# A fused attention and two mixture layers on one core: more loads in flight at once, and a new order and engine choice under that plan

## The chip, the cores and the metric

The kernel runs on one core of a Trainium2 chip. The metric is the device time of the whole kernel in microseconds (us). A profiled execution also gives the span: the time from the first to the last recorded instruction. The core has TensorE (PE; its weight loads are listed as PEld), VectorE (DVE), ScalarE (ACT), GpSimd (POOL) and SyncE (SP), which in this kernel issues every transfer; the transfers run on 16 DMA engines.

## The reference

```python
# 1. attention, q, k, v of (4, 8, 576, 64), two results added
q_d, k_d, v_d = means of q, k, v over 4 neighbouring tokens        # 144 tokens
out_up    = repeat(softmax(q_d @ k_d.T / 8) @ v_d, 4)
out_local = softmax(q @ k.T / 8 where |i - j| < 4) @ v
x = out_up + out_local                                             # as 2304 tokens x 512
# 2. a layer with a rational function
h = x @ w_in                                                       # 512 -> 2048
P = a[0] + a[1] * h + a[2] * h * h + a[3] * h * h * h
Q = 1.0 + abs(b[0]) * abs(h) + abs(b[1]) * h * h
x = (P / (Q + 1e-06)) @ w_out                                      # 2048 -> 512
# 3. soft mixture of 8 experts, 4 slots each
logits = x @ phi                                                   # 32 slots
slot_input = softmax(logits, over the tokens).T @ x
slot_out   = relu(slot_input @ w1[e]) @ w2[e]                      # 8 experts, 512 -> 1024 -> 512
out = softmax(logits, over the slots) @ slot_out
```

The softmax over the tokens needs all 2304 tokens before the first expert can start, so the experts form a tail behind everything else.

## The kernel before

**Stages.** The attention is done for 16 pairs of heads (four batches of four). A pair needs one load of its q and k (`in_qk`, 579 KB, all 128 partitions) and two of v, always issued one behind the other: `in_vd` (320 KB, for the means) and `in_vw` (560 KB, windows for the local part). There are four sets of buffers. The first batch uses all four; the later pairs wait for one to come free. A pair's q and k are summed over four tokens (L560 on VectorE, or L562 and twice L564 on POOL), its scores are multiplied (L580 local, L590 means), their maxima taken (L595), the exponentials done (ScalarE), divided by their sums (L617), turned, multiplied with v (L643), and added (L667). v is summed by L570 and L571. The result x is split into a high half XH (L729 on ScalarE or L731 on VectorE) and a low half XL = x - XH (L734), because TensorE's products take the rounded type and are made as high x high, high x low and low x high.

The weights `w_in` and `w_out` come as 64-bit floats, eight loads of 1024 KB each, and are narrowed to 32 bits on VectorE (L756, L761, L765). Each part of `w_in` is split into W high and low (the same L729, L731 and L734). Each part of `w_out` is stored as 32 bits to a scratch in DRAM (`wo_dram`, 512 KB), to be loaded again in the tail, and multiplied by phi, so that the logits come straight from the gate.

Products m = 0 to 31 (24 matmuls each, L889) multiply 512 tokens with 256 columns of `w_in`; m = 32 to 35 (L907, 48 matmuls each) do the last 256 tokens with 512 columns. Product m needs XH and XL of its batch and W of its part, and it writes into one of two pairs of PSUM banks, m modulo 2. So product 2 needs the banks that the gate of product 0 has read. A gate is a chain of some ten instructions on 128 x 1024 values: L965 to L994 on ScalarE, VectorE and POOL; the last is L994. Its result is turned (L1018), copied (L729 or L731), and goes into the logits (L1034), and once per 256 tokens into the slots (L1090). The experts follow (L1330, L1451) with 32 loads `we` of 1024 KB, which are issued as buffers come free.

The other loads are two constants at the start, `in_cb` (117.5 KB) and `in_cf` (195 KB).

**What sets the order.** The program is written by a planner. `at` collects items (a part's name, what it reads and writes); every item has a number in the table `PLACE`, and `simulated` (L321) goes through the items in the order of these numbers, so the numbers alone set the order on every engine. For several kinds of item, a letter in the table `F` says which engine takes each instance: d is VectorE, p is POOL, a, s and r are ScalarE, and f is VectorE too, with another place for a result (see g below). The letters of the parts: `pq`, `pk`, `pv` are the sums of q, k, v; `nl`, `nd` are L617; `wil` is the low half of W, `xl` of x; `cr`, `v`, `a`, `t` are steps of the gate (`cr` and `a` are L967 if not on ScalarE, `v` and `t` are L971); `g` = f writes the last but one value of the gate over PSUM, where d writes it to SBUF; `gc` is the copy after L1018.

`simulated` also gives each item a time, from the table of costs `PARTS`. These times decide three things in the program that is built. First, loads are throttled: for a load of the front (`GATED`, q and k, v, `w_in`, `w_out`), it goes back over the loads ahead and adds up their planned durations until `LIMIT` is reached; the load then waits for the landing of the one at which it got there (L352 to L358, built in `begin`, L425). Second, a wait of TensorE that is planned longer than 0.6 us is filled with dummy matmuls (L386; `fillers`, L1157: wide ones at L1159, narrow ones at L1162). Third, of certain instructions on POOL and VectorE the plan lets only one engine's run at a time, and a POOL instruction that is planned right behind one of VectorE waits for it in the program (L434). When a load's data may be used in the plan is `end[n]` at L363; the program itself waits for the data and not for that time.

```python
for m in reversed(loads if part in GATED else ()):
    if ahead >= LIMIT:
        t, self.gate[n] = max(t, end[m] + .1), m
        break
    ahead += items[m][2][0]
```

## Time and profile before

| | |
|---|---|
| time, median of 3 runs | 506.7 us (501.92 to 507.81) |
| profiled execution, its time | 502.77 us |
| profiled execution, span | 501.0 us |
| busy: TensorE | 474.4 us (95%) |
| busy: VectorE | 399.7 us (80%) |
| busy: ScalarE | 322.1 us (64%) |
| busy: GpSimd | 250.6 us (50%) |
| moved by DMA | 88.50 MB, mean 177 GB/s |

The busy times are of the profiled execution. Dummy matmuls count as busy TensorE. The rows that follow the diff come from this execution; a row of a timeline gives the start, the duration, the engine, the line, the operation, what goes out and in, and in brackets how long the engine was idle before it and who released it.

### The profile page before, as it was taken

The page shows a single profiled execution, that of the slowest core. Times are in us where ns is not written, and L with a number is a line of the kernel's source. Part 1 is how long each engine was busy: PE and PEld are TensorE (multiplying, and loading weights), DVE is VectorE, ACT ScalarE, POOL GpSimd, SP SyncE. Part 2 cuts the span into 40 slices and gives each one's busy share as a digit, 9 for nine tenths or more (in the row PEclk, how much of TensorE's full clock was granted, in tenths as well). Part 3 has the DMA queues.
Part 4 walks back from the last instruction along what each step waited for, and adds up shares of the span by engine and source line. Part 5 has one row for each costly group of instructions (what it writes and reads, how often), then busy time and mean ns, then how long its engine had stood idle before and what let it go on. Part 6 is the DMA issues. An engine that isn't in the chain of part 4 may idle for free.

```text
span 501.0 us, 13108 instructions
## 1 busy us (share of the span) xinstructions
PE 474.4 (95%) x5505; PEld 345.4 (69%) x5505; DVE 399.7 (80%) x558; ACT 322.1 (64%) x676; POOL 250.6 (50%) x223
## 2 busy tenths in 40 slices
PE   8798699999999999999999999999989989999995
PEld 5576477677777777766777777777766878543575
DVE  5985989998997888889978988889879988825333
ACT  4584297686968887568688667869585567720223
POOL 3786579466883775575154376723544134301000
PEclk9799799999999999999999999999999999999998
DMA  8997816477654220144301222660202049999988
GB/s 318 296 316 249 301 49 169 160 207 246 211 160 126 47 67 7 41 123 121 104 18 38 86 75 75 205 262 0 85 0 63 22 152 386 381 404 426 427 336 306
DMA packets 17611, 88.50 MB, mean 177 GB/s; under 512 B 2065, under 2 KB 2577, under 8 KB 10897
## 3 DMA queue, kind: packets, MB, share of 16 engines
q1 hardware_dynamic: 17552, 87.67, 50.3%
q8 instruction: 43, 0.70, 0.6%
q14 instruction: 16, 0.12, 0.1%
HBM read 78.75 MB, written 8.91 MB: 175 GB/s over the span
## 4 chain that ended last, share of the span: by engine, by line
PE 50%; DVE 17%; DMA 13%; POOL 8%; ACT 6%; issue 4%; SPq 0%; DVEq 0%; POOLq 0%; ACTq 0%
PE hps L889 18%; DMA at<-in_vw 4%; POOL gate L971 4%; PE gt L1018 4%; PE op L1451 3%; DMA wo_dram<-wo 3%; DVE gate L990 3%; PE hp L1330 3%; POOL W L734 2%; PE lg L1034 2%; PE hps L907 2%; ACT hps L989 2%; PE dsp L1090 2%; DMA wst<-in_w_out 2%; PE av L643 2%
## 5 line engine op out<-in xcount | busy, mean ns | idle before, releaser
L889 PE MATMUL hps<-XH,W 128*128 128x512 f32 x512 | 170.1, 402 | 7.4 <-ACT XH L729 3.0
L889 PEld LDWEIGHTS hps<-XH,W 128*128 128x128 f32 x512 | 97.1, 190 | 33.8 <-ACT XH L729 3.2
L971 POOL TENSOR_TENSOR gate<-gate 128x1024 f32<-128x1024 f32 (+1 forms) x37 | 86.4, 2335 | 59.1 <-ACT gate L976 41.4
L889 PE MATMUL hps<-XL,W 128*128 128x512 f32 x256 | 100.9, 394 | 1.3 <-POOL XL L734 1.3
L967 POOL TENSOR_SCALAR gate<-gate,cf_sb 128x1024 f32<-128x1024 f32 (+1 forms) x25 | 30.7, 1229 | 78.6 <-ACT gate L975 78.6
L990 DVE SCALAR_TENSOR_TENSOR gate<-gate,hps 128x1024 f32<-128x1024 f32 (+1 forms) x37 | 44.0, 1190 | 23.3 <-ACT hps L989 21.3
L988 ACT ACTIVATE gate<-gate,one 128x1024 f32<-128x1024 f32 (+1 forms) x37 | 42.1, 1138 | 29.6 <-POOL gate L971 29.3
L889 PEld LDWEIGHTS hps<-XL,W 128*128 128x128 f32 x256 | 48.6, 190 | 10.8 <-POOL XL L734 1.8
L989 ACT ACTIVATE hps<-gate 128x1024 f32<-128x1024 f32 (+1 forms) x37 | 37.4, 1010 | 14.9 <-DVE gate L987 7.7
L729 ACT COPY G<-gt 128x512 f32<-128x512 f32 x50 | 29.3, 588 | 6.6 <-PE gt L1018 6.5
L1159 PE MATMUL lg<-zero 128*96 128x256 f32 x114 | 31.8, 420 | 1.0 <-DVE zero L1154 1.0
L971 DVE TENSOR_TENSOR gate<-gate,hps 128x1024 f32<-128x1024 f32 x24 | 29.0, 1209 | 3.7 <-ACT gate L965 3.7
L975 ACT ACTIVATE gate<-hps 128x1024 f32<-128x1024 f32 (+1 forms) x26 | 25.9, 996 | 8.2 <-PE hps L889 7.7
L1018 PE MATMUL gt<-cf_sb,gate 128*128 128x128 f32 x192 | 28.7, 279 | 1.3 <-ACT DC L1084 0.9
L994 DVE SCALAR_TENSOR_TENSOR gate<-gate 128x1024 f32<-128x1024 f32 x17 | 28.3, 1663 | 0.4
L965 ACT ACTIVATE gate<-hps,cf_sb 128x1024 f32<-128x1024 f32 x23 | 27.9, 1212 | 1.1 <-PE lg L1034 1.1
L987 DVE SCALAR_TENSOR_TENSOR gate<-gate,cf_sb,hps 128x1024 f32<-128x1024 f32 x22 | 28.0, 1275 | 0.5
L602 ACT ACTIVATE at<-sc,at 128x38 f32<-128x38 f32 x144 | 28.1, 316 | 0.5
L756 DVE TENSOR_SCALAR nar<-wst 128x512 int32<-128x512 int32 (+1 forms) x26 | 21.0, 812 | 8.5 <-DMA wst<-in_w_in 6.2
L617 POOL TENSOR_TENSOR at<-at 128x342 f32<-128x342 f32 (+1 forms) x29 | 23.9, 834 | 6.2 <-DVE at L613 3.7
L1018 PEld LDWEIGHTS gt<-cf_sb,gate 128*128 128x128 f32 x192 | 21.3, 141 | 8.2 <-issue 3.6
L1159 PEld LDWEIGHTS lg<-zero 128*96 128x96 f32 x114 | 19.3, 179 | 10.7 <-issue 3.9
(177 smaller groups left out, 1018.0 us busy)
## 6 DMA issues: line engine op xcount, KB each, us to landing
we<-in_w SPq DMA_DIRECT2D x32, 1024.0 KB, 12.4
at<-in_qk SPq DMA_DIRECT2D x16, 579.0 KB, 4.8
at<-in_vw SPq DMA_DIRECT2D x16, 560.0 KB, 6.4
wst<-in_w_in SPq DMA_DIRECT2D x8, 1024.0 KB, 6.7
wst<-in_w_out SPq DMA_DIRECT2D x8, 1024.0 KB, 6.1
at<-in_vd SPq DMA_DIRECT2D x16, 320.0 KB, 5.0
out<-late SPq DMA_DIRECT2D x17, 256.0 KB, 2.7
wo_dram<-wo SPq DMA_DIRECT2D x8, 512.0 KB, 7.3
```

The lines of the kernel that those rows point to most:

```text
L602: nc.scalar.activation(out=dst[:, i, :], in_=st["s", j][:, i, :], func=ACTF.Exp, scale=scale, bias=mx[:, i:i + 1], accum_out=None if sums ...
L729: nc.scalar.copy(out=out, in_=x)
L889: nc.tensor.matmul(hps[m][:, c].rearrange("p u t -> p (u t)"), lhsT=W[p][:, w, kk, 128 * c:128 * c + 128], rhs=x[xx][:, kk, :], start=(kk ...
L967: (nc.vector if who == "d" else nc.gpsimd).tensor_scalar(out=out, in0=x, scalar1=coef[:, w:w + 1], scalar2=coef[:, b:b + 1], op0=ALU.mult, ...
L971: turned_over((nc.vector if who == "d" else nc.gpsimd).tensor_tensor(out=out, in0=x, in1=y, op=op), who)
L987: stt(out=A, in0=A, scalar=coef[:, 1:2], in1=H, op0=ALU.add, op1=ALU.mult))
L988: do("ln", "C", "B", lambda C, B: act(out=C, in_=B, func=ACTF.Ln, bias=one))
L989: do("ex", "H", "C", lambda H, C: act(out=H, in_=C, func=ACTF.Exp, scale=-1.0))
L990: do("e", "B", "H", lambda B, H: stt(out=B, in0=B, scalar=1.0 + 1e-6, in1=H, op0=ALU.add, op1=ALU.mult))
L994: do("g", "A", "B" + n, lambda A, B, n: turned_over(stt(out=A, in0=B, scalar=-2.0, in1=n, op0=ALU.add, op1=ALU.mult), "d"), pick=("g", m))
L1018: nc.tensor.transpose(gt[n][:, u, 128 * c:128 * c + 128], g_of(n, c)[:, 128 * u:128 * u + 128], idn)
L1159: nc.tensor.matmul(fill[0:96], lhsT=wide, rhs=wide[:, 0:1].to_broadcast([128, TB]), start=not used, stop=True, skip_group_check=True)
```

## The change

`LIMIT` goes from 2.6 to 4.5, the planned time from a transfer's end to the use of its data goes from 0.5 to 0.9, and the table `PLACE` (all of it) and fifteen strings of `F` are new. Nothing else in the program is touched.

```diff
-    pq="dppddpppppdpdddp",
-    pk="ddppppppdpppdpdd",
-    pv="pppppppppppppppp",
-    nl="ppppppppppppppdp",
-    nd="pppppppppppddppp",
+    pq="dppppppppdpppppp",
+    pk="pddppppppppppppp",
+    pv="pppppppppdpdpppp",
+    nl="ppppppppddddppdp",
+    nd="pppppppppdppdppd",
     wih="aaaaaaad",
-    wil="pppppppp",
-    xh="aaaaaadaddaaaaaaa",
-    xl="ppppppppddpppppdp",
-    cr="aspppspssppppppssspppppsspppsppsppppa",
-    t="dpddppddddddddddddddddddddddddddddddd",
-    sd="rsssrsrsrsrrrsss",
-    v="ppppppppppppppppppppppppppppppppppppp",
-    a="aaaaaaaaaaaaaadaaaaaddaaaaaaaaaaaaaaa",
-    g="fdfddffddfdddfddddfddddddddddddddffff",
-    gc="aaaadaaadaadaaaadaaaaddaaadadaaddaaadaaaadaddadaaadaadadadadadaaaaaaaada",
+    wil="pppppppd",
+    xh="aaaaaaaadadadadda",
+    xl="ppppdpdddpppddddd",
+    cr="spppspppppppssppaappdpppppssspappsppa",
+    t="dpdpddddddddddddddddpdddddddddddddddd",
+    sd="rsssssrrssrsssrs",
+    v="pppppppppppppppppdppdppppppppppppdppp",
+    a="aaaaaadaaadaaaaaaaaaaaaaadaaaddaaadaa",
+    g="ddfdfffddddddddddddddffddddddddddddff",
+    gc="aaaaaaaaaadddaaaaadaaaaadadadadaaaaaadadadaadaaaaaaaaaadaadaaaadaaaaadaa",
...
-    ldi=(11, 27, 109, 113, 151, 189, 192, 205),
...
+    ldi=(15, 57, 93, 117, 145, 192, 169, 201),
...
-BACK, LIMIT, GATED = 2.5, 2.6, ("ldqk", "ldv", "ldi", "ldo")
+BACK, LIMIT, GATED = 2.5, 4.5, ("ldqk", "ldv", "ldi", "ldo")
...
-                end[n] = moved + .5
+                end[n] = moved + .9
```

Counted over the strings and the orders of both programs, VectorE gets seven L734 (five XL, the low half of the last W, the low half of the last 256 tokens), five L617, two pairs L570/L571, four L967 and three L971 from other engines, and gives away nine L560 and four L731.

**SP, the loads of the front.** The rows are the stretch around the last v loads of the first batch. at_89 and at_87, at_103 and at_101, at_96 and at_94 are the two v loads of a pair, wst the 64-bit weights, and at_86 the q and k of the fifth pair of heads. Before:

```order
L427 DMA wst_523<-in_w_out 128x2048
L427 DMA wo_dram_71<-wo_423 128x1024
L427 DMA wst_567<-in_w_in 128x2048
L427 DMA at_89<-in_vd 80x1024
L427 DMA at_87<-in_vw 112x1280
L427 DMA wst_577<-in_w_in 128x2048
L427 DMA at_96<-in_vd 80x1024
L427 DMA at_94<-in_vw 112x1280
L427 DMA wst_690<-in_w_in 128x2048
L427 DMA wo_dram_71<-wo_631 128x1024
L427 DMA at_86<-in_qk 128x1158
```

And now:

```order
L427 DMA at_89<-in_vd 80x1024
L427 DMA at_87<-in_vw 112x1280
L427 DMA wst_449<-in_w_out 128x2048
L427 DMA at_103<-in_vd 80x1024
L427 DMA at_101<-in_vw 112x1280
L427 DMA wo_dram_71<-wo_429 128x1024
L427 DMA wst_520<-in_w_in 128x2048
L427 DMA wst_578<-in_w_in 128x2048
L427 DMA at_86<-in_qk 128x1158
L427 DMA wst_642<-in_w_in 128x2048
L427 DMA at_96<-in_vd 80x1024
L427 DMA at_94<-in_vw 112x1280
```

The last pair of v loads (at_96, at_94) stood behind two `w_in` of this piece, with a third `w_in` and the fifth pair's q and k behind it; now the third `w_in` and these q and k stand ahead of it.

**POOL, from the low half of W2 on to that of W4.** XL is the low half of x, at_102, at_88 and at_95 are x of three of the four pairs of the first batch, and L562, L564 sum the q or the k of one of the next pairs. Before:

```order
L734 TENSOR_TENSOR W2_750<-wst_567,W2_750 128x1024
L734 TENSOR_TENSOR XL_544<-at_88,XH_521 128x512
L562 TENSOR_TENSOR at_88<-at_86 128x144
L564 TENSOR_TENSOR at_88<-at_88,at_86 128x144 x2
L734 TENSOR_TENSOR XL_544<-at_95,XH_521 128x512
L734 TENSOR_TENSOR W3_849<-wst_577,W3_849 128x1024
L734 TENSOR_TENSOR W4_891<-wst_690,W4_891 128x1024
```

And now:

```order
L734 TENSOR_TENSOR W2_645<-wst_520,W2_645 128x1024
L562 TENSOR_TENSOR at_88<-at_86 128x144
L564 TENSOR_TENSOR at_88<-at_88,at_86 128x144 x2
L570 TENSOR_TENSOR at_96<-at_96 72x512
L571 TENSOR_TENSOR at_93<-at_96 72x256
L734 TENSOR_TENSOR XL_542<-at_102,XH_540 128x512
L734 TENSOR_TENSOR W3_790<-wst_578,W3_790 128x1024
L734 TENSOR_TENSOR XL_542<-at_88,XH_540 128x512
L734 TENSOR_TENSOR XL_542<-at_95,XH_540 128x512
L734 TENSOR_TENSOR W4_869<-wst_642,W4_869 128x1024
```

The sums at_88 stood between two XL of the first batch, and now stand ahead of all three; one XL more and the sums of v (L570, L571) have come into this piece, and W3 stands ahead of the last two XL.

**TensorE, between the products 1 and 2.** lg<-zero are the fillers, L576 to L590 are the scores of the fifth pair, L832 and L842 the products of `w_out` with phi. Before, the rows right behind the last matmul of product 1:

```order
L1159 MATMUL lg_73<-zero_114 96x256 x5
L842 MATMUL wq_926<-cf_sb_74,pp_580 128x32 x2
L1159 MATMUL lg_73<-zero_114 96x256 x5
L576 LDWEIGHTS cb_sb_75
L576 MATMUL sc_942<-cb_sb_75 128x342
L580 MATMUL sc_942<-at_86 32x38 x36
L832 MATMUL wp_995<-wo_631,cf_sb_74 32x256 x4
L1159 MATMUL lg_73<-zero_114 96x256 x5
L1162 LDWEIGHTS zero_114
L1162 MATMUL lg_73<-zero_114 96x192
L590 MATMUL scd_1006<-at_88 64x144 x6
L1159 MATMUL lg_73<-zero_114 96x256 x7
```

And now, the rows up to the first matmul of product 2 (hps_1011):

```order
L576 LDWEIGHTS cb_sb_75
L576 MATMUL sc_934<-cb_sb_75 128x342
L580 MATMUL sc_934<-at_86 32x38 x36
L832 MATMUL wp_975<-wo_580,cf_sb_74 32x256 x4
L1159 MATMUL lg_73<-zero_114 96x256 x5
L1162 LDWEIGHTS zero_114
L1162 MATMUL lg_73<-zero_114 96x192
L842 MATMUL wq_1002<-cf_sb_74,pp_994 128x32 x2
L1159 MATMUL lg_73<-zero_114 96x256
L889 MATMUL hps_1011<-XH_540,W2_645 128x512
```

Where 22 wide fillers stood in four lots behind product 1 (the turn of the first gate, L1018, and product 2 follow a few narrow ones later), there are six now, and two more stand some rows ahead, inside product 1. The scores L590 of the fifth pair have moved ahead of the end of product 1.

## Rows read from the trace of the kernel before

**Rows 1.** The page: busy tenths in 40 slices of the span, one engine.
```profile
PE   8798699999999999999999999999989989999995
```

**Rows 2.** By stretch: length; PE, PEld, DVE, ACT, POOL busy; clock, DMA share, GB/s.
```profile
0.00:46.30 46.30, 39.11 (x700) 28.49 (x701) 36.59 (x64) 27.66 (x97) 30.84 (x49) 0.93 0.90 294
...
0.00:78.50 78.50, 66.78 (x971) 48.90 (x972) 62.31 (x108) 45.59 (x125) 52.03 (x61) 0.91 0.74 246
78.50:394.20 315.70, 310.31 (x3493) 231.56 (x3491) 275.78 (x343) 233.53 (x475) 178.93 (x151) 1.00 0.34 107
440.00:480.00 40.00, 38.50 (x430) 18.50 (x432) 14.09 (x50) 6.52 (x16) 1.86 (x1) 1.00 1.01 424
```

**Rows 3.** The same by stretch, line L1159 alone: PE, PEld, clock, DMA share, GB/s.
```profile
0.00:78.50 78.50, 23.00 (x82) 14.67 (x82) 0.91 0.74 246
```

**Rows 4.** The same by stretch, fillers of both widths: PE, clock, DMA share, GB/s.
```profile
0.00:78.50 78.50, 24.24 (x95) 0.91 0.74 246
78.50:394.20 315.70, 5.91 (x27) 1.00 0.34 107
```

**Rows 5.** Loads issued on SP (count, first and last start), and the last one's time to landing.
```profile
L427 SPq DMA_DIRECT2D we<-in_w x32: 327/332/729, 318.6 to 467.2; - x32
...
L427 SPq DMA_DIRECT2D wst<-in_w_in x8: 328/328/347, 2.8 to 57.0; - x8
...
wst<-in_w_in SPq DMA_DIRECT2D x1, 1024.0 KB, 5.2
```

**Rows 6.** Timeline of TensorE: the first matmuls of product 2 and of product 32.
```profile
78.55 0.48 PE L889 MATMUL hps<-XH,W 128*128 128x512 f32 x1
...
394.24 1.46 PE L907 MATMUL hps<-xs,W 128*128 128x256 f32 x10 [0.18 <-DVE gate L993]
```

**Rows 7.** VectorE by stretch, then three places of its timeline.
```profile
0.00:78.00 78.00, 61.81 (x107) 0.91 0.75 247
...
5.10 2.21 DVE L560 TENSOR_REDUCE at<-at 128x144 f32<-128x576 f32 x3 [3.57 <-DMA at<-in_qk]
...
50.60 0.69 DVE L756 TENSOR_SCALAR nar<-wst 128x512 int32<-128x512 int32 x1 [4.07 <-DMA wst<-in_w_in]
...
76.80 1.22 DVE L994 SCALAR_TENSOR_TENSOR gate<-gate,hps 128x1024 f32<-128x1024 f32 x1
```

**Rows 8.** Timeline of POOL.
```profile
47.17 1.08 POOL L734 TENSOR_TENSOR XL<-at,XH 128x512 fp32r<-128x512 f32 x1
...
54.68 0.56 POOL L562 TENSOR_TENSOR at<-at 128x144 f32<-128x144 f32 x1 [6.42 <-DMA at<-in_qk]
...
56.51 1.09 POOL L734 TENSOR_TENSOR XL<-at,XH 128x512 fp32r<-128x512 f32 x1
```

**Rows 9.** The chain that ended last, in order of time: start, share of it in us.
```profile
31.31 7.92 DMA at<-in_vw
39.60 6.66 DMA at<-in_vw
```

**Rows 10.** Timeline of VectorE, two of its XL.
```profile
210.87 0.69 DVE L734 TENSOR_TENSOR XL<-at,XH 128x512 fp32r<-128x512 f32 x1
...
324.63 2.45 DVE L734 TENSOR_TENSOR XL<-at,XH 128x512 fp32r<-128x512 f32 x1 [0.55 <-ACT XH L729]
```

**Rows 11.** Groups by line and form: busy us, mean ns of one | idle before.
```profile
L971 DVE TENSOR_TENSOR gate<-gate,hps 128x1024 f32<-128x1024 f32 x24 | 29.0, 1209 | 3.7 <-ACT gate L965 3.7
...
L734 POOL TENSOR_TENSOR W<-wst,W 128x1024 fp32r<-128x1024 f32 x8 | 19.4, 2424 | 4.2 <-ACT W L729 3.4 <-DVE W L731 0.8
L731 DVE COPY G<-gt 128x512 f32<-128x512 f32 x22 | 15.0, 684 | 0.9 <-PE gt L1018 0.8
...
L967 DVE TENSOR_SCALAR gate<-hps,cf_sb 128x1024 f32<-128x1024 f32 x1 | 1.3, 1334 | 0.0
```

**Rows 12.** VectorE by stretch around the small instructions on the coefficients: busy, clock, DMA share.
```profile
19.40:21.10 1.70, 1.63 (x9) 0.70 0.98 242
54.70:56.10 1.40, 1.23 (x8) 0.50 0.89 193
```

More of the change, by code (lines that the diff above doesn't have):

```diff
@@ L160 @@
[L160 to L176 removed]
+    dm=(8,),
@@ new lines @@
+    ldqk=(4, 7, 31, 5, 125, 252, 361, 452, 546, 592, 716, 795, 822, 941, 1027, 1069),
+    ldc=(6, 0),
+    ldv=(42, 76, 163, 72, 219, 413, 466, 551, 602, 722, 800, 862, 944, 1063, 1092, 1176),
+    coef=(1,),
+    roots=(2,),
+    rooted=(3,),
+    pq=(9, 25, 58, 22, 149, 285, 412, 465, 580, 638, 726, 806, 842, 942, 1031, 1117),
+    pk=(10, 21, 81, 16, 174, 335, 383, 453, 554, 617, 748, 796, 858, 960, 1033, 1134),
+    sc=(17, 24, 44, 27, 236, 331, 437, 510, 585, 634, 744, 816, 895, 972, 1040, 1116),
@@ new lines @@
+    w1=(34, 62, 90, 112, 133, 150, 161, 178, 204, 198, 207, 187, 217, 227, 269, 279, 313, 318, 362, 357, 407, 409,
+        449, 469, 542, 547),
+    w2=(46, 63, 109, 118, 134, 165, 164, 179, 205, 200, 214, 191, 225, 230, 276, 281, 314, 319, 363, 369, 414, 420,
+        455, 470, 545, 548),
+    wih=(73, 114, 147, 184, 210, 218, 232, 244),
+    wil=(98, 122, 154, 189, 216, 224, 239, 245),
+    ldo=(20, 74, 246, 294, 327, 387, 436, 492),
+    sto=(80, 235, 282, 349, 405, 450, 500, 628),
+    wt0=(95, 231, 288, 330, 370, 435, 496, 565),
@@ new lines @@
+    wc0=(96, 237, 291, 333, 374, 438, 497, 570),
+    wt1=(88, 128, 292, 326, 379, 424, 503, 562),
+    wc1=(89, 131, 297, 339, 382, 425, 507, 566),
+    wp=(102, 240, 300, 340, 396, 441, 518, 588),
+    wpp=(105, 253, 308, 345, 397, 445, 522, 607),
+    wq=(120, 254, 321, 364, 415, 509, 557, 608),
+    wpc=(121, 257, 324, 367, 419, 513, 563, 619),
+    h=(113, 202, 212, 213, 177, 197, 222, 233, 262, 260, 315, 303, 351, 348, 410, 381, 447, 456, 532, 543, 597, 595,
+        615, 614, 649, 651, 676, 669, 710, 712, 747, 749, 781, 784, 826, 846, 912, 908, 918, 919, 955, 958, 991, 994,
+        1013, 1020, 1048, 1056, 1093, 1090, 1160, 1149, 1197, 1195, 1222, 1221, 1238, 1243, 1259, 1261, 1289, 1288,
+        1299, 1301, 1329, 1325, 1341, 1344),
@@ new lines @@
+    L=(665, 847, 965, 1049, 1256, 1322, 1429, 1477, 1513),
+    mx=(675, 834, 968, 1061, 1251, 1314, 1437, 1471, 1517),
+    al=(733, 874, 1018, 1147, 1278, 1328, 1454, 1479, 1525),
+    E=(692, 848, 1030, 1153, 1266, 1330, 1450, 1482, 1519),
+    ss=(736, 1017, 1034, 1260, 1313, 1355, 1472, 1510, 1528),
+    tk=(729, 849, 1042, 1173, 1277, 1338, 1452, 1483, 1520),
+    dt=(730, 852, 1044, 1174, 1279, 1347, 1459, 1484, 1522),
+    ds=(807, 872, 1045, 1185, 1296, 1350, 1464, 1485, 1523),
+    ac=(810, 880, 1047, 1207, 1297, 1357, 1467, 1499, 1526),
@@ new lines @@
+    wor=(1194,),
+    h8=(1366, 1367, 1365, 1369, 1384, 1385, 1387, 1388, 1420, 1421, 1417, 1418, 1433, 1434, 1441, 1447),
+    we=(1224, 1411, 1391, 1368, 1371, 1489, 1508, 1487, 1509, 1386, 1389, 1422, 1419, 1435, 1449, 1448, 1540, 1542,
+        1524, 1515, 1533, 1555, 1551, 1553, 1549, 1562, 1564, 1569, 1567, 1572, 1580, 1575),
+    zm=(1415,),
+    gst=(1527,),
+    inv=(1529,),
+    gt0=(1530,),
+    gt1=(1531,),
+    sl=(1532,),
+    si0=(1534,),
+    si1=(1535,),
+    si=(1536,),
+    z=(1537,),
@@ L187 @@
[L187 to L193 removed]
+    c2=(1545,),
+    c3=(1546,),
+    cs=(1548, 1560, 1558, 1552, 1563),
+    ct=(1557, 1561, 1583, 1577, 1571),
+    cc=(1566, 1568, 1592, 1582, 1573),
@@ new lines @@
+    l2=(1578, 1579, 1581, 1584, 1585, 1586, 1587, 1588, 1590, 1591, 1594, 1603, 1604, 1610, 1616, 1619, 1597, 1598,
+        1613, 1620, 1627, 1635, 1636, 1644),
+    os=(1589, 1629, 1648),
+    s4=(1593, 1633, 1649),
+    s4h=(1595, 1637, 1650),
+    s4l=(1596, 1638, 1653),
+    o=(1609, 1599, 1606, 1614, 1600, 1612, 1617, 1626, 1624, 1639, 1642, 1647, 1654, 1656, 1658, 1662, 1669, 1665,
+        1667),
+    out=(1623, 1607, 1621, 1625, 1602, 1630, 1632, 1641, 1631, 1645, 1646, 1652, 1657, 1661, 1664, 1666, 1673, 1672,
+        1674),
```

197 lines of the change are left out of this document (65 added, 132 removed), and 14 rows, old and new, of tables (gc, tr).

## The prediction

> **What bounds the kernel now.** I read the page first, then the engines by stretch, then the waits of the front, then the filler matmuls. The slices [rows 1] show TensorE busy nearly everywhere. That row is to be distrusted, because the plan puts dummy matmuls (L1159, L1162) into TensorE's planned waits. The stretches [rows 2] and the fillers alone [rows 3, 4] correct it. Up to 78.5 us TensorE is busy for 66.8 us, but 24.2 of them are fillers of both widths [rows 4], most of them wide [rows 3]: it does 42.5 us of work, and 36 us are waiting, filled or not. From 78.5 to 394.2 us it waits 5.4 us (315.7 less 310.31) and burns 5.9 us of fillers [rows 4]: 11.3 us in 315.7, so this stretch belongs to TensorE, with VectorE close behind at 275.8 us (87%). Behind 394.2 us the loads of the last weights decide: DMA is busy throughout between 440 and 480 us, at 424 GB/s [rows 2], and the last of the 32 loads is issued only at 467.2 us [rows 5].
>
> So the place to look is the front, up to the moment when product 2 starts (78.55 us [rows 6]), just after the first gate is finished (the L994 that begins at 76.80 us [rows 7]). Three things stand there. DMA is the slower side until the last input weight has landed (the eighth load of in_w_in is issued at 57.0 us and takes 5.2, so 62.2 [rows 5]), but busy for only 90% of the first 46.3 us [rows 2]. VectorE works 61.8 of the first 78.0 us [rows 7] and so waits 16.2 us, the longest time 4.07 us for an input weight [rows 7]. And POOL waits 6.42 us at L562 for the q and k of the fifth head pair, with the last XL of the first batch (56.51 us, needed by products 0 and 1) queued behind it [rows 8].
>
> **The loads.** LIMIT goes from 2.6 to 4.5, so a 1 MB load waits for the third load before it instead of the second. The bytes hardly change. What must have moved when the last in_vw of the front lands (39.60 + 6.66, 46.3 us [rows 9]) is, by the sizes in the section on the kernel and the order of SP: before, cb and cf, 4 in_qk, 4 in_w_in, 2 in_w_out, 4 v pairs, one store, 12,804 KB; now one in_w_in and one in_qk more, 14,407 KB, 12.5% more. At the old pace that is 52.1 us; with the DMA never idle (share 0.90 up to 46.3 us [rows 2]) it is 52.1 x 0.90 = 46.9 us. Neither is shown, so I take the middle, 49.5 us, and keep both ends. The same for the last input weight: 17,479 KB in place of 17,991, so 60.4 us at the old pace, 54.4 without idle, 57 taken, against 62.2. A v load needed 9 us from landing (31.31 + 7.92) to the end of its XL (47.17 + 1.08) [rows 8, 9], which gives the last XL at 58.5 us against 57.6 now. The order of POOL keeps the fifth pair's L562 ahead of XL, but its load now stands ahead of the last v, so XL waits for its own data and no more for that one.
>
> **VectorE up to product 2.** The order shows 105 instructions ahead of the first L994 both times: two L560 fewer (three took 2.21 at the start [rows 7], 0.74 each), one L595 more (taken as much as one of them), and the low half of W7 on VectorE, which no row has; twice an XL of 0.69 [rows 10] is 1.4, and POOL's 2.42 for it [rows 11] is the upper end. Together -0.74 + 1.4, +0.7. Against that, the first gate no longer writes into the PSUM of product 0 (g is "d", not "f"), so product 2 needs not wait for L994 itself, 1.22 us. VectorE thus has 61.8 + 0.7 - 1.2 = 61.3 us to do. Its waits: 16.2 now. Thirteen small instructions on the coefficients (1.63 and 1.23 us of VectorE with a neighbour's share, taken as 2.6 [rows 12]) move from busy places to the start, where VectorE waits for its first q and k anyway; and I let half of the 4.07 us wait go. That leaves 16.2 - 2.6 - 2.0 = 11.6, so product 2 starts at 72.9, say 73: **5.5 us won**. Ends: 8 won if the whole 4.07 goes and the DMA never idles; 2 if it keeps the old pace and XL ends at 61. The fillers between products 1 and 2 fall from 22 wide ones to 8 in the order; 14 at 0.56 us (82 records in 23.00 us [rows 3]; a filler is two of them, so 41) are 7.9 us, much the same. I do not count that again.
>
> **From product 2 to product 32.** The order has no filler left between them, 5.9 us before. It also has more VectorE work there, by [rows 11] unless said: three L971 (1.21), four L967 (1.33), five XL (0.69 [rows 10]), five L617 (taken like an XL), W7 and xs (two XL each, 1.4), two value poolings L570/L571 (no row on VectorE, 1.4 each likewise), less nine L560 (0.74) and four copies of L731 (0.68): 3.6 + 5.3 + 3.5 + 3.5 + 2.8 + 2.8 - 6.7 - 2.7 = 12 us, most of it taken from POOL. It lies beside TensorE's work: VectorE goes from 275.8 of 315.7 us to some 288 of 312, 92%. That cover is thin, so I let 1.9 of the 5.9 us come back as waits: **4 us won**. Ends: 5.9 won; or all 12 us in series less the 5.9, 6.1 lost.
>
> What a moved instruction can cost beside a busy POOL is shown by one of them: an XL on VectorE took 0.69 us at 210.87 and 2.45 at 324.63 [rows 10], 1.76 more. The Trainium skill ("GPSIMD Engine Reference", section Key points) states that GpSimd shares its SBUF interfaces with VectorE, with contention for VectorE instructions that have two SBUF inputs. By that, all 16 moved instructions of that kind could be stretched, 16 x 1.76 = 28 us, and the forecast would turn into a loss; the trace agrees that it happens, but for one XL in three.
>
> **The tail.** From product 32 (394.24 us [rows 6]) to the end are 106.8 us, set by the load stream at 2.5 us per MB. SP now issues w0 and w1 right after the first products 32, but o0 and o1, which before were loaded ahead, come later too. One load either way is 2.5 us; I take **0**, ends +2.5 and -2.5.
>
> **The sum.** The profiled execution took 502.77 us, 501.0 of them span. 502.8 - 5.5 - 4 = 493.3. The median of the runs shown is 506.7, 3.9 above that execution, so the same gain on the median gives 497.2. I predict the middle, 495. The three runs lie 1.2% apart, so 2%, about 10 us, is what a measurement can tell from no change.
>
> **Rivals.**
> A, the forecast: 9.5 us won, 495.
> B, the waits of the front nearly vanish. VectorE then waits only at the start (its first L560 begins at 5.10 us [rows 7]; 6 us in all): product 2 at 67, 11 won, plus the full 5.9: 502.8 - 11 - 5.9, 486 on the scale of the profiled execution. For it: 41 wide fillers ahead of product 2 become 19. Against: DMA was already busy for 90% of 46 us, and the order is no clock.
> C, the load stays where it was: XL at 61, 2 us won in front, and the 12 us on VectorE eat the fillers: 501 to 505. For it: VectorE is at 92%, and 12.5% more bytes stand ahead of the last v.
> D, slower: VectorE becomes the bound of the middle. Of the 16 moved two-operand instructions half meet a busy POOL, 8 x 1.76 = 14 us, and with the 12 us that is 26 in series. TensorE's 11.3 us of waits absorb the first part, the front's 5.5 the next: 26 - 11.3 - 5.5 is 9.2 us lost, 512. It decides from 16.8 us on, that is, from three or four stretched instructions in series. For it: the 2.45 us; against: TensorE waited only 5.4 us in that stretch while VectorE was at 87%.
>
> **How the numbers follow.** A 0.42, B 0.17, C 0.27, D 0.14. The forecast lies just beyond 2%, so two thirds of A and all of B count as faster: 0.45. The rest of A and nearly all of C are within 2%: 0.42. D is slower: 0.13. The range 484 to 512 holds A with its ends, B, C and D up to its price.
>
> **What would show it.** Right: product 2 starts near 73; the last in_vw lands near 49 and the last in_w_in near 57; POOL's 6.4 us wait at L562 is gone or short; fillers after 78 us only in the tail; VectorE's waits up to the first L994 at 11 to 12 us; the stretch from product 2 to product 32 near 312 us. Wrong: product 2 at 77 or later (then the loads were not the cause), VectorE's mean for L734, L617 or L994 well above the present ones, or a stretch from product 32 to the end that is more than 3 us off 106.8.

## The result, and the profile after

The changed kernel takes 496.35 us, the median of four executions (495.88 to 498.27), against 506.78 (501.92 to 507.81) of the kernel before: ratio 0.9865, interval 0.9826 to 0.9905, so faster by 1.0 to 1.7%, which is less than the 2% that the prediction called the least that a measurement can tell. The four executions of before lie high: beside the later runs its medians were 502.59 (19 executions), 502.83 (19), 503.65 (7) and 502.64 (10), some 6 to 7 us above the changed kernel and not 10. The profiled execution took 496.0 us with a span of 494.2, 6.8 less than the span of before. The forecast was 495, with 5.5 us won up to product 2, 4 in the middle and nothing in the tail; the rows below give 4.5, 5.8 and a loss of 3.5.

The page's slices of TensorE, against [rows 1]:

```profile
PE   7677889999999999999999999999999999799994
```

The engines by stretch, columns as in [rows 2], each stretch ended where the same thing happens as in before: the last in_vw landed, the last in_w_in landed, product 2, product 32, the end.

```profile
0.00:51.10 51.10, 36.96 (x679) 26.36 (x680) 38.01 (x71) 27.36 (x97) 35.06 (x57) 0.89 0.97 308
0.00:61.10 61.10, 46.94 (x787) 33.80 (x788) 47.00 (x89) 30.98 (x102) 43.12 (x62) 0.89 0.97 311
0.00:74.00 74.00, 58.00 (x918) 41.21 (x918) 59.80 (x105) 42.48 (x116) 51.75 (x66) 0.91 0.84 268
74.00:383.90 309.90, 304.57 (x3464) 228.68 (x3463) 279.04 (x355) 234.38 (x489) 177.60 (x155) 1.00 0.31 101
383.90:494.20 110.30, 97.77 (x1036) 65.17 (x1036) 62.12 (x110) 44.31 (x78) 17.45 (x11) 0.97 0.85 339
```

The fillers by the same stretches (PE, clock, DMA share, GB/s), against [rows 4]:

```profile
0.00:74.00 74.00, 13.10 (x41) 0.91 0.84 268
74.00:383.90 309.90, 0.00 (x1) 1.00 0.31 101
383.90:494.00 110.10, 3.93 (x16) 0.97 0.86 340
```

Product 2 starts 4.5 us earlier (78.55 to 74.03), the stretch from there to product 32 is 5.8 us shorter (315.7 to 309.9), and the tail 3.5 us longer (106.8 to 110.3). That adds up to the 6.8 us. The DMA is no longer idle in front (share 0.97 up to 51.1 us, 0.90 up to 46.3 before), but what it brings lands late, as the issues on SP and their times to landing show:

```profile
38.53 0.47 SPq L427 DMA_DIRECT2D at<-in_vw  x1
...
at<-in_vw SPq DMA_DIRECT2D x1, 560.0 KB, 12.6
...
51.16 0.33 SPq L427 DMA_DIRECT2D wst<-in_w_in  x1
...
wst<-in_w_in SPq DMA_DIRECT2D x1, 1024.0 KB, 9.9
```

The last v of the front took 12.6 us instead of 6.66 [rows 9], with four other loads under way when it was issued, and landed at 51.1; the last input weight took 9.9 instead of 5.2 [rows 5] and landed at 61.1, just 1.1 us earlier than before.

The timeline at product 2:

```profile
74.03 0.50 PE L889 MATMUL hps<-XH,W 128*128 128x512 f32 x1
...
74.32 1.78 DVE L994 SCALAR_TENSOR_TENSOR gate<-gate 128x1024 f32<-128x1024 f32 x1
```

The first L994 now starts behind product 2, not ahead of it as in [rows 6, 7].

What comes ahead of that is not data that arrive earlier, but the order on ScalarE. ScalarE reads product 0 for the first time (L975) at 62.22 us before and at 62.27 now, so product 0 is no earlier. From there to product 2 it was 16.3 us and is 11.8. Before, with the first L975 and the L965 whose result VectorE's L971 takes:

```profile
62.22 1.03 ACT L975 ACTIVATE gate<-hps 128x1024 f32<-128x1024 f32 x1 [1.07 <-PE hps L889]
...
68.19 1.24 ACT L965 ACTIVATE gate<-hps,cf_sb 128x1024 f32<-128x1024 f32 x1
```

And now:

```profile
62.27 1.11 ACT L975 ACTIVATE gate<-hps,cf_sb 128x1024 f32<-128x1024 f32 x1
63.28 1.10 ACT L976 ACTIVATE gate<-hps,turns 128x1024 f32<-128x1024 f32 x1
64.28 1.20 ACT L965 ACTIVATE gate<-hps,cf_sb 128x1024 f32<-128x1024 f32 x1
```

Before, two steps of the second gate (L975 at 64.97, L976 at 66.99) and the high half of a W stood in ScalarE's order ahead of that L965; now the first gate's three steps follow each other. VectorE's L971 starts at 66.12 instead of 69.56 us and its L990 at 71.57 instead of 74.35, 2.8 us earlier; the rest of the 4.5 us is L994, which product 2 no longer waits for.

One more milestone is needed to read this rightly. Product 3 starts at 85.51 us, against 87.80: only 2.3 us earlier. Of the 4.5 us at product 2, half is given back within one product, where VectorE is busy all the time (the row of 74.00 in the next fence). From product 3 to product 32, 8.0 us are won.

```profile
74.00:85.50 11.50, 10.40 (x67) 7.41 (x66) 11.29 (x16) 9.46 (x27) 8.77 (x8) 1.00 0.55 203
85.50:383.90 298.40, 294.17 (x3401) 221.27 (x3397) 267.75 (x340) 224.92 (x463) 168.84 (x147) 1.00 0.31 97
```

The rows of before are these, product 2 to 3 and product 3 to 32:

```profile
78.55:87.80 9.25, 9.05 (x59) 7.08 (x58) 8.75 (x14) 7.16 (x14) 8.85 (x12) 1.00 0.72 213
87.80:394.20 306.40, 301.20 (x3437) 224.43 (x3434) 266.98 (x329) 226.37 (x462) 170.03 (x140) 1.00 0.33 104
```

### The profile page after: what moved, and what is told of

It is laid out like the page before. It is cut to its first block, busy times and chain, and to the rows that moved or that the text cites. A ratio compares the mean times of both kernels' runs of the same rounds, so it can differ in the third digit from the quotient of the medians.

```text
span 494.2 us, 12949 instructions
## 1 busy us (share of the span) xinstructions
PE 460.3 (93%) x5417; PEld 335.1 (68%) x5417; DVE 401.0 (81%) x568; ACT 321.2 (65%) x682; POOL 246.8 (50%) x231
## 4 chain that ended last, share of the span: by engine, by line
PE 42%; DVE 21%; POOL 12%; ACT 11%; DMA 9%; issue 4%; SPq 0%; DVEq 0%; POOLq 0%; ACTq 0%
PE hps L889 15%; POOL gate L971 7%; DMA at<-in_qk 5%; PE op L1451 3%; DVE gate L990 3%; ACT hps L989 3%; PE gt L1018 3%; PE hps L907 2%; DMA wst<-in_w_in 2%; POOL gate L967 2%; ACT gate L988 2%; DMA wo_dram<-wo 2%; ACT gate L975 2%; PE hp L1330 2%; PE scd L590 2%
## 5 line engine op out<-in xcount | busy, mean ns | idle before, releaser
L889 PE MATMUL hps<-XH,W 128*128 128x512 f32 x512 | 169.4, 400 | 2.4 <-DVE wst L765 1.8
L889 PEld LDWEIGHTS hps<-XH,W 128*128 128x128 f32 x512 | 96.6, 189 | 28.8 <-issue 2.5
L971 POOL TENSOR_TENSOR gate<-gate 128x1024 f32<-128x1024 f32 (+1 forms) x34 | 81.1, 2386 | 47.1 <-ACT gate L965 21.9
L889 PE MATMUL hps<-XL,W 128*128 128x512 f32 x256 | 100.7, 393 | 0.2
L967 POOL TENSOR_SCALAR gate<-gate,cf_sb 128x1024 f32<-128x1024 f32 (+1 forms) x25 | 32.2, 1289 | 71.9 <-ACT gate L975 70.4
L990 DVE SCALAR_TENSOR_TENSOR gate<-gate,hps 128x1024 f32<-128x1024 f32 (+1 forms) x37 | 44.0, 1188 | 14.0 <-ACT hps L989 13.5
L889 PEld LDWEIGHTS hps<-XL,W 128*128 128x128 f32 x256 | 48.4, 189 | 9.8 <-POOL XL L734 0.9
L729 ACT COPY G<-gt 128x512 f32<-128x512 f32 x56 | 32.7, 590 | 9.7 <-PE gt L1018 9.4
L564 POOL TENSOR_TENSOR at<-at 128x144 f32<-128x144 f32 x56 | 35.5, 634 | 4.4
L975 ACT ACTIVATE gate<-hps 128x1024 f32<-128x1024 f32 (+1 forms) x29 | 29.0, 999 | 5.4 <-PE hps L889 4.2
L971 DVE TENSOR_TENSOR gate<-gate,hps 128x1024 f32<-128x1024 f32 x24 | 29.1, 1214 | 4.0 <-ACT gate L965 3.8
L1018 PE MATMUL gt<-cf_sb,gate 128*128 128x128 f32 x192 | 28.7, 278 | 2.5 <-ACT G L729 1.1
L1018 PEld LDWEIGHTS gt<-cf_sb,gate 128*128 128x128 f32 x192 | 21.7, 141 | 11.3 <-ACT G L729 3.8
L987 DVE SCALAR_TENSOR_TENSOR gate<-gate,cf_sb,hps 128x1024 f32<-128x1024 f32 x22 | 28.1, 1276 | 0.6
L994 DVE SCALAR_TENSOR_TENSOR gate<-gate 128x1024 f32<-128x1024 f32 x20 | 26.0, 1298 | 0.4
L617 POOL TENSOR_TENSOR at<-at 128x432 f32<-128x432 f32 (+1 forms) x24 | 20.3, 852 | 12.0 <-DVE at L613 8.7
L965 ACT ACTIVATE gate<-hps,cf_sb 128x1024 f32<-128x1024 f32 x19 | 23.0, 1208 | 4.0 <-PE gt L1018 2.6
L907 PE MATMUL hps<-xs,W 128*128 128x256 f32 x192 | 24.3, 285 | 1.3 <-DVE A L993 1.2
L993 DVE SCALAR_TENSOR_TENSOR gate<-gate,cf_sb,hps 128x1024 f32<-128x1024 f32 x20 | 25.5, 1273 | 0.0
```

The source lines that it names most:

```text
L564: nc.gpsimd.tensor_tensor(out=dst, in0=dst, in1=x[:, :, j], op=ALU.add)
L729: nc.scalar.copy(out=out, in_=x)
L889: nc.tensor.matmul(hps[m][:, c].rearrange("p u t -> p (u t)"), lhsT=W[p][:, w, kk, 128 * c:128 * c + 128], rhs=x[xx][:, kk, :], start=(kk ...
L907: nc.tensor.matmul(out[:, c, :], lhsT=W[p][:, w, kk, 128 * c:128 * c + 128], rhs=xs[i][:, xx, kk, :], start=(kk == 0 and j == 0), stop=(kk ...
L967: (nc.vector if who == "d" else nc.gpsimd).tensor_scalar(out=out, in0=x, scalar1=coef[:, w:w + 1], scalar2=coef[:, b:b + 1], op0=ALU.mult, ...
L971: turned_over((nc.vector if who == "d" else nc.gpsimd).tensor_tensor(out=out, in0=x, in1=y, op=op), who)
```

## The experiments

In all of them the edit is made in the kernel of before or in the changed one, as the expectation says. Starts of products are those of the first matmul of L889 or L907 in the timeline.

**How deep the queue of loads is (three runs).** The plan's own times stay, so order, engines and fillers do too; only which landing a load waits for changes:

```diff
-                loads.append(n)
+                self.gate[n] = ([m for j, m in enumerate(loads) if sum(items[k][2][0] for k in loads[j + 1:]) >= 2.6][-1:] or [None])[0] if part in GATED else None; loads.append(n)
```

with 2.6 in the changed kernel, 4.5 in the kernel before, and 7.0 in the changed kernel without fillers.

> The changed kernel, its order, engines and fillers untouched, but each load of the front waits by the old rule (2.6 in place of 4.5). Theory A, the depth of the queue is what brings product 2 forward: product 2 starts at 76 to 78.5 us instead of 74.0, and the whole is 2 to 4.5 us longer than the changed kernel (498.5 to 501). Rival, the new order and engine choice do it and the depth is worth nothing: product 2 at 73 to 75, the whole within 1 us of the changed kernel. Second rival, the deeper queue only shares the same DMA among more loads: product 2 earlier than 73.

> The kernel before, its order, engines and fillers untouched, but each load of the front waits by the new rule (4.5 in place of 2.6). Theory A: product 2 starts 2 to 4 us earlier than 78.55, at 74.5 to 76.5, and the last input weight lands at 57 to 60 us instead of 62.2. Rival: product 2 within 1 us of 78.55. Second rival: with more loads sharing the DMA the last v of the front lands later than 46.3 by 2 us or more, and product 2 with it, at 79.5 or later.

> The changed kernel without fillers, with a load of the front waiting by 7.0 in place of 4.5, so with one more load in flight; everything else untouched. Theory A (depth brings product 2 forward): product 2 at 71 to 73 us, where the same program at 4.5 showed 73.2, 74.3 and 75.4 in three executions, and the whole 1 to 2 us below 493.7. Rival, the DMA is busy anyway (97% up to 61 us) and more loads in flight only share it: product 2 at 73 to 76, the whole within 1.5 us. Second rival, the sharing delays what is needed first: product 2 later than 76.

Measured: in the old order, with the deeper queue, product 2 starts at 75.26 us, where three programs of before with the old rule show 78.55, 78.20 and 78.96 (the second and third are the run without fillers and the one with guarded gates, below); the ratio to before is 0.9948, interval 0.9911 to 0.9986, so 0.7 to 4.5 us of the 502.6. Product 3 follows at 84.48, so none of it is given back there. The last input weight landed at 58.6 us (62.2 in the kernel before, 60.3 and 60.9 in the other two), and the last v of the front at 46.1, no later than before; the first is as theory A has it, the second not as the second rival has it. But the granted clock was higher too: 0.98 up to product 2 in this execution, against 0.91 before, and 0.988 on the mean of its ten executions, against 0.983 of the nineteen of before. A line through those nineteen gives 4.2 us per 0.01 of clock; by this estimate the clock goes with 1.8 of the 1.9 us by which the means differ. Whether the queue raised the clock or the clock alone made the gain, no run separates. In the new order the shallow queue gives product 2 at 75.69 instead of 74.03, between the ranges of theory A and of the rival, and the same whole as the rival has it: 496.21 us against 496.35. That difference at product 2 is within the scatter: one and the same program up to product 32 gave 73.15, 74.31, 75.41 and 75.62 in four of the executions below, and the changed kernel's own front gave 72.66 in the run that keeps its fillers there. The still deeper queue gives 76.26, by that the second rival's, and 494.79 us, no gain over 493.68. So the depth won nothing in the new order, and that it won something in the old one is likely but not shown.

What does tell the fronts apart is the time from ScalarE's first reading of product 0 to product 2: 11.3 to 13.2 us in the eight executions with the new front, 16.3 to 18.8 in the four with the old front and its letters. The first reading itself is no earlier with the new front (60.9 to 64.9 us) than with the old one (58.2 to 62.2). So the front's gain is order and engine choice, and not loads.

**Fillers (three runs).** The edit, in the kernel before, in the changed one, and in the changed one behind product 32 alone:

```diff
-    plan.idle = fillers
+    plan.idle = lambda n, w=0: None
```

```diff
-    plan.idle = fillers
+    plan.idle = lambda n, w=0: fillers(n, w) if plan.items[plan.item][0] < 1365 else None
```

> The kernel before without any filler behind the first twenty. Theory A, which counted 5.9 us of fillers between product 2 and product 32 as time that comes back when they go: this stretch falls from 315.7 us to 310 to 312, and the whole by 4 to 6 us. Rival, fillers lie in waits that are there with or without them: the stretch stays at 314.5 to 316.5, with the waits in place of the fillers, and the whole within 1.5 us. In the front the same question: product 2 at 78.55 or within 1 us of it by the rival, at 76 or earlier if fillers hold TensorE back there. If the clock falls where fillers stood, the rows of the granted clock show it, and the stretch is longer.

> The changed kernel without any filler behind the first twenty. By theory A fillers cost time only between product 2 and 32, where this kernel has none left: that stretch 309.9 us within 1, product 2 at 74.0 within 1, the tail within 1 of 110.3. Rival: the 13.1 us of fillers ahead of product 2 keep TensorE's clock up, and without them it falls to its lower level for longer: product 2 later than 75.

> The changed kernel with its fillers ahead of product 2 and without the few behind product 35. If fillers cost time in the tail, where the plan's waits are shorter than planned: the tail 106.5 to 108.3 us in place of 110.3 (58.2 us to the first L1330 becomes 57.7), the upper end if the clock falls in the expert stage again. The front as in the changed kernel: product 2 at 73.5 to 75, product 3 at 85 to 87, and the whole 492 to 494.5. Rival, the fillers of the tail cost nothing and its length is the clock's alone: 109.5 or more, the whole within 1 us of 496.

Measured in the kernel before: 500.9 us, ratio 0.9958 (0.9924 to 0.9992). Product 2 to product 32 takes 313.2 us instead of 315.7: 2.5 us come back, not the 5.9 that the fillers took and not nothing. The front stays (78.20), so 24.2 us of fillers there cost almost nothing: they lay in waits that stay. (In this run TensorE was at half clock for 20.5 of the first 78.2 us, 13.7 before, and product 2 came no later.)

In the changed kernel without any: 493.68 us, ratio 0.9786 (0.9721 to 0.9850), the lowest median of all runs. The middle does not move (310.06), as it has no fillers. The tail is 108.3 us in place of 110.3, and 106.4 in the run that keeps those of the front:

```profile
383.90:490.20 106.30, 93.47 (x1020) 62.56 (x1020) 62.07 (x110) 44.22 (x78) 17.43 (x11) 0.98 0.89 352
```

That last run took 494.99 us, ratio 0.9857 (0.9805 to 0.9909), just above the range expected; its product 2 and 3 (72.66 and 84.14) lie just below theirs. The three versions without all or some of the fillers (493.68, 494.79 with the still deeper queue, 494.99) can't be told apart, and their intervals touch that of the changed kernel itself.

**What the stretched L994 cost (one run).** The groups of L994 on VectorE by form showed in the kernel before what the page does not: those with two inputs in SBUF took 1.66 and 1.72 us, those with one in PSUM (hps) 1.22.

```profile
L994 DVE SCALAR_TENSOR_TENSOR gate<-gate 128x1024 f32<-128x1024 f32 x17 | 28.3, 1663 | 0.4
...
L994 DVE SCALAR_TENSOR_TENSOR A<-gate,A 128x1024 f32<-128x1024 f32 x9 | 15.5, 1724 | 0.2
...
L994 DVE SCALAR_TENSOR_TENSOR gate<-gate,hps 128x1024 f32<-128x1024 f32 x7 | 8.5, 1221 | 0.2
```

The timeline shows who stretched them: six met an L971 of POOL and took 3.34, 2.83, 2.42, 3.25, 3.24 and 3.03 us. One of them, and one with PSUM input in the same position:

```profile
375.24 2.40 POOL L971 TENSOR_TENSOR gate<-gate 128x1024 f32<-128x1024 f32 x1
...
375.47 3.25 DVE L994 SCALAR_TENSOR_TENSOR gate<-gate 128x1024 f32<-128x1024 f32 x1
...
182.20 2.38 POOL L971 TENSOR_TENSOR gate<-gate 128x1024 f32<-128x1024 f32 x1
...
182.05 1.22 DVE L994 SCALAR_TENSOR_TENSOR gate<-gate,hps 128x1024 f32<-128x1024 f32 x1
```

POOL's instruction keeps its 2.4 us; VectorE's ends 1.1 us behind it (377.64 and 378.72), so of its 3.25 us some 2.0 are more than the 1.22 of an undisturbed one. It goes the other way too: in the changed kernel an L994 starts at 205.44 us, takes 1.21, and the L971 of POOL that starts behind it at 205.64 takes 3.27. The Trainium skill ("Trainium Architecture — The Big Picture", section What this means for kernel authors) calls this shared port pair an exclusive lock and no split of bandwidth; by these rows that holds. In the changed kernel no L994 with two SBUF inputs between product 3 and product 32 takes over 1.4 us (the rows are of the whole kernel, with one of 1.78 us ahead of product 3 and one of 2.03 behind product 32):

```profile
L994 DVE SCALAR_TENSOR_TENSOR gate<-gate 128x1024 f32<-128x1024 f32 x20 | 26.0, 1298 | 0.4
...
L994 DVE SCALAR_TENSOR_TENSOR A<-gate,A 128x1024 f32<-128x1024 f32 x9 | 11.0, 1219 | 0.1
```

The experiment takes the stretch out of the kernel before (without fillers), by letting the six L971 wait for the L994 that they met; four numbers of v in the order go behind those of g, which moves nothing on POOL:

```diff
+            z = (nc.vector if who == "d" else nc.gpsimd).tensor_tensor(out=out, in0=x, in1=y, op=op); turned_over(z, who)
+            if m in LATE and who == "p" and op != ALU.subtract: tc.add_manual_dep(z.ins, ends[m - 1].ins.name, GATE, reason="behind L994")
```

> The kernel before without fillers, its order on every engine untouched; six L971 on POOL (v of the products 2, 4, 15, 29, 30, 31), which ran beside an L994 of VectorE that was stretched to 2.4 to 3.3 us, now wait for the end of that L994. If the stretched L994 are what the middle lost: the mean of the L994 with both inputs in SBUF falls from 1.65 to 1.35 us or less, VectorE does 6 to 10 us less, and product 2 to product 32 falls from 313.2 to 309.5 to 311.5. Rival, the stretch costs nothing on the path, or POOL's later start costs as much as it gives: the mean falls and the stretch stays at 312.5 to 314.

Measured: the means fall to 1.22 and 1.37 us:

```profile
L994 DVE SCALAR_TENSOR_TENSOR gate<-gate 128x1024 f32<-128x1024 f32 x17 | 20.7, 1219 | 0.4
L994 DVE SCALAR_TENSOR_TENSOR A<-gate,A 128x1024 f32<-128x1024 f32 x9 | 12.3, 1365 | 0.2
```

Product 2 to product 32 is 312.6 us, by the expectation the rival's. But its rows show that product 2 to 3 ran at a granted clock of 0.79, which the run without fillers did not have. Product 2 to 3 and 3 to 32, first without fillers, then with the guard too:

```profile
78.20:87.60 9.40, 9.27 (x59) 7.06 (x57) 8.68 (x13) 7.34 (x14) 9.00 (x12) 1.00 0.68 205
87.60:391.40 303.80, 296.48 (x3409) 220.62 (x3408) 266.93 (x330) 226.12 (x462) 169.85 (x140) 1.00 0.33 105
```

```profile
78.96:90.50 11.54, 11.34 (x58) 8.72 (x57) 9.46 (x14) 7.15 (x14) 9.40 (x11) 0.79 0.74 229
90.50:391.50 301.00, 295.99 (x3410) 220.65 (x3407) 257.51 (x328) 226.49 (x462) 168.80 (x139) 1.00 0.33 103
```

From product 3 on, at full clock in both, VectorE has 9.4 us less to do and the stretch is 2.8 us shorter (303.8 to 301.0). So under a third of the stretched time lay on the path; the rest was hidden. This starting point was chosen after the result; by the expectation's own stretch the run is the rival's. That the 2.8 us are the guards' is borne out by where they lie: 1.5 us between the products 28 and 32 (35.90 us in both kernels of before, 34.36 here, 33.12 in the changed one) and 1.2 between 3 and 5 (23.68 to 22.53); product 5 to product 28, with one guarded L994 in it, is the same within 0.1 us. The whole is 498.57 us, ratio 0.9857 (0.9815 to 0.9899), below the interval of the run without fillers alone (0.9924 to 0.9992).

**Letters without their order, and the order without the old front (two runs).** Without fillers; first all fifteen strings of F from the changed kernel in the kernel before, then the changed kernel with the items up to product 2 in the order of before and the old load rule.

```diff
-    xl="ppppppppddpppppdp",
+    xl="ppppdpdddpppddddd",
...
```

> The kernel before, its order and load rule, with all fifteen strings of engine letters from the changed kernel, and no fillers; to be compared with the kernel before without fillers (product 2 at 78.2, 313.2 us to product 32) and the changed one without fillers (73.2 and 310.1). Theory L, the letters give the 3 us of the middle: 309.5 to 311.5 us. Theory O, the new order does, and the letters alone only load VectorE: 313 to 319. In front the letters alone (g of the first gate among them, 1.2 us): product 2 at 76.5 to 77.5; if it stays at 78 the gate was not what was waited for.

> No fillers, the new letters, the old load rule; every item up to product 2 in the order of before, everything from there on in the new order. Against the run with the new letters alone only the order behind product 2 differs. Theory O: the middle is 309 to 311 us, as in the changed kernel, while the run with the letters alone is over 313. Theory L: both within 1 us of each other. Third possibility, the middle profits from what the front leaves behind (attention pairs done earlier): then it is over 312 here although its order is new.

Measured: the letters alone make the kernel 7% slower, 540.61 us, ratio 1.0718 (1.0608 to 1.0828). Both theories are wrong: product 2 comes at 79.87, though its gate writes to SBUF now, and the middle takes 341.8 us:

```profile
79.90:421.70 341.80, 316.84 (x3466) 233.19 (x3464) 284.46 (x353) 232.42 (x481) 168.56 (x151) 0.97 0.31 96
```

No engine is busy throughout there: VectorE works 284 of 342 us, and TensorE waits 25 us (341.8 less 316.84) instead of 5.3 in the changed kernel. So this order loses with another choice of engines. With the new order behind product 2 as well, product 2 starts late (83.04), but the middle takes 310.3 us, 299.06 of them from product 3 on: the gain of the middle belongs to the order and letters of the middle, and is no gift of the front. The whole is 501.07 us, ratio 0.9938 (0.9896 to 0.9979), 7.4 us above the changed kernel without fillers: the old front doesn't fit the new letters either. In these two runs it is 21.5 and 22.3 us from ScalarE's first reading of product 0 to product 2.

**The tail (three runs).** Without fillers: everything from product 32 on in the order of before; the same with the letters of before there; and the new tail with 28 loads instead of 32.

```diff
+        if (layer, j) == (2, 2):
+            for c in range(2):
+                we[2, 2, e + c] = we[2, 1, e + c]
+            return
```

> The changed kernel without fillers, with everything from product 32 on in the order of the kernel before. The tail was 106.4 us in the order of before and 108.3 in the new order, both without fillers. If the order of the tail makes the difference: 106 to 107, and the whole 1.5 to 2.5 us below the changed kernel without fillers (493.7), at 491 to 492. If it is the clock, which falls at 459.5 us in the new tail and not in the old, whatever the order, or the loads: 108 or more.

> The changed kernel without fillers, with everything from product 32 on in the order of the kernel before, and now also with the engine letters of before for what stands there (cr and v of product 33, a of 34, g of 33 and 34, seven copies gc). The order alone, with the letters of the changed kernel, had made the tail 114.8 us. If the order of the tail with its own letters is the better one: tail 106 to 107 us, of which 20.7 us are from the first to the last of L1451 in place of 22.8 to 23.3; the whole 490 to 492.5. If the tail is longer for another reason (what the middle leaves behind): 108 or more, the whole 493 or more.

> The changed kernel without fillers and without the last four of the 32 loads of expert weights; the second layer uses the tiles of the four before them in their place, so this part of the computation is another one, with the same instructions. 4 MB less at the 2.5 us per MB of the forecast. The forecast's step, the load stream sets the tail: 108.3 us falls by 4 to 10 us. Rival, TensorE's own work sets it and the loads are ahead of it: 108.3 within 0.8 us.

Measured: the old order alone gives a tail of 114.8 us (106 to 107 expected) and 504.24 us in all, again because letters and order don't fit (cr, v, a and g of two products and seven copies); two stretches of 3.4 us at half clock lie in this tail too. With its letters it gives 106.1 and 495.5 us, as expected of the tail, but above the range for the whole, as product 2 came at 75.62. The load stream does not set the tail: with 4 MB less, the last load issued at 447.5 instead of 454.0 us (rows of the issues, the changed kernel and then this run), it is 108.4 us (one execution) against 108.3 without fillers, both with the stretch at half clock that is shown below. In the kernel before this was not tried.

```profile
L427 SPq DMA_DIRECT2D we<-in_w x32: 327/328/430, 325.3 to 454.0; - x32
```

```profile
L427 SPq DMA_DIRECT2D we<-in_w x28: 327/328/2114, 327.5 to 447.5; - x28
```

What made the new tail 3.5 us longer can be read by its parts: product 32 to the first L1330 57.6 us before and 58.2 now, to the first L1451 18.2 and 18.7, to the end of L1451 20.7 and 22.8, to the end of the span 10.2 and 10.5. In the run without fillers in the tail these are 57.7, 18.5, 21.6 and 8.6. The third part contains a stretch at half clock that neither the kernel before nor that run has (busy PE, clock, DMA share, GB/s; the stretch and the four microseconds ahead of it):

```profile
456.00:460.00 4.00, 3.64 (x31) 1.00 1.01 426
460.00:463.40 3.40, 3.40 (x29) 0.50 1.00 424
```

Three executions of the new tail show such a stretch (here, at 459.5 in the run without fillers, at 462.2 in the one with four loads less): 22.8 to 23.3 us for the part. Four don't: 21.6. Sorted by both, the seven executions of the new tail give the whole answer: at full clock 106.4 to 106.6 us without fillers and 108.2 with them, with the stretch at half clock 108.3 and 108.4 without and 110.3 with them. The tail of before takes 106.4 us without fillers, 106.7 and 106.8 with them. So of the 3.5 us some 1.7 are fillers and 1.8 the clock, and the order costs nothing: what it loses up to the end of L1451 (0.9 and 0.2 us) it gains behind it. There the new tail ends 0.9 to 1.9 us sooner without fillers than with them (8.6 to 9.0 against 9.9 and 10.5); the last store is issued 0.4 us behind its copy where it was 1.6 in the changed kernel. Why is open, and so is why the clock falls in some executions.

## Why the prediction was right, and where it wasn't

The direction, the time (495 for 496.35) and the order of size of both gains were right; the single steps are a mixed lot, and that the time is so near is in part luck. On the scale of the profiled executions 9.5 us were forecast and 6.8 measured; 495 was the middle between that scale and a median of four high executions. Of the chances, the 0.42 for "within 2%" came true and not the 0.45 for faster. Of the prediction's own signs of being wrong one came: the tail is more than 3 us off.

- **Product 2 at 73, 5.5 us won: 74.03, 4.5 won.** VectorE had 59.8 us to do (61.3 taken) and waited 14.2 (11.6 taken): its work fell by 2.5 us and its waits by 2.0, where the sum took 0.5 and 4.6, so two errors cancel. The sum also did not see where the time was won: behind ScalarE's first reading of product 0, by the order there, and by no earlier data. That product 2 would no longer wait for L994 itself is confirmed by the timeline, 74.03 against 74.32. The wait for an input weight shrank to 2.0 us at its longest (4.07 before), as taken.
- **Loads: mis-sized.** "57 taken" for the last input weight was 61.1, outside both ends; the last v at 51.1 was within 46.9 to 52.1, but not at 49.5. The step that failed is the count of bytes that stand ahead in the order: with more loads in flight, bytes that stand behind move at the same time. By the row, 308 GB/s times 51.1 us is 15.7 MB, where the order had 14,407 KB of 1024 bytes, 14.75 MB, ahead; before it was 13.6 MB with 13.1 ahead. The DMA did become busy (0.97), as the lower ends assumed; it just worked for later loads too. The last XL of the first batch still ended at 58.8 us, near the forecast (58.5), by luck: its load came 1.6 us later and it followed 7.7 us behind its load and not 9; POOL's 6.42 us wait at L562 [rows 8] is gone from there.

```profile
57.72 1.09 POOL L734 TENSOR_TENSOR XL<-at,XH 128x512 fp32r<-128x512 f32 x1 [0.56 <-ACT XH L729]
```

- **The milestone.** Product 2 was the wrong place to end the front. Half of its gain was gone at product 3, where VectorE is the bound (11.29 of 11.50 us). The sum came out because the gain behind it was larger than forecast.
- **Middle: 4 us forecast, 5.8 measured, 8.0 from product 3 on, for other reasons.** "I let 1.9 of the 5.9 us come back as waits" was too hopeful: without fillers the kernel before gains 2.5 there. Guarded L994 add 2.8 (303.8 to 301.0); that the changed kernel, whose L994 are not stretched there, gains as much by it is argued from this run of the old order. The last 2.6, to 298.4, are order and letters that no run took apart.
- **VectorE's 12 us: right, and yet not what it did.** Summed by line over 78.5 to 394.2 and 74.0 to 383.9 us, L734, L967, L617, L971 and L570/L571 gained 4.5, 4.2, 3.5, 2.6 and 3.1 us and L560 lost 5.2: 12.7. (W7 and two of the nine L560 were counted both here and up to product 2; they lie ahead of product 2 and nearly cancel. The L731 that went gave nothing back: 21 took 13.7 us, 18 take 13.9.) But L994 lost 8.3 at the same time (29 of mean 1.57 to 30 of mean 1.24), so VectorE's busy time rose only from 275.8 to 279.0 us. The rows of L994 by form stood in the trace of before, and the prediction did not look at them.
- **Rival D fell** on the price: the XL on VectorE took 0.89 us on the mean, 0.2 more than an undisturbed one [rows 10], not 1.76.

```profile
L734 DVE TENSOR_TENSOR XL<-at,XH 128x512 fp32r<-128x512 f32 x8 | 7.1, 892 | 0.1
```

  The stretching is real, and I looked for it on the moved instructions alone. Where it cost most, on L994, it went by the order: the six L971 that stretched L994 before are on POOL in the changed kernel too. Only one L971 of POOL still meets an L994 with two SBUF inputs between the products 3 and 32, and as it starts second there, it is the one that waits (3.27 us). The new letters alone, in the old order, do not remove the stretch: there the two groups of L994 take 1.50 and 1.86 us.
- **Tail: wrong.** "Set by the load stream at 2.5 us per MB" failed: four loads less change nothing (108.4 against 108.3). In the kernel before I took a DMA that is busy throughout for the bound; TensorE was as busy there, 38.50 of 40 us [rows 2]. The term was 0 with 2.5 either way, and measured 3.5 longer: fillers and half clock, neither of which the term had, and nothing from order or loads.
- **Rivals B and C.** B's full return of the fillers fell with the run without them (2.5 of 5.9). C had the last input weight right, late as before, but not XL at 61, and not the price: product 2 gained 4.5 us all the same, by ScalarE's order, and the 12 us of VectorE did not eat the rest.

## What to carry to other kernels

What a filler costs depends on where it stands: in the stretch that belongs to TensorE 2.5 of 5.9 us came back when they went, in the front hardly any of 24, in the new tail some 1.7 of 3.9. When a product starts earlier, look whether its data came earlier or whether the engine that reads them got to it sooner: here an L965 that stood behind two steps of another gate was worth more than the loads. Before you give VectorE more work, list its instructions with two SBUF inputs by form and see which of them are stretched by one of GpSimd beside them; an order in which they don't meet took 8.3 us of VectorE's work away here, two thirds of the 12.7 that came. An order and its choice of engines belong together (new letters in the old order cost 7%, the old front with the new letters 7.4 us): try them together, and put the end of a stage where the next bound begins, not at the first matmul that starts early.
